# Casting transfers for the first quarter of w_in and for v of batches 3 to 7 in an attention-then-MLP kernel

## The chip, the cores and the metric

The kernel runs on one core of one Trainium2 chip. The metric is the device time of one execution in microseconds (us). Three executions of the kernel before took 284.15, 283.83 and 285.68 us, with a median of 284.15. Batches are counted from 0 here, as in the code: the "fourth to eighth batch" are b = 3 to 7.

The engines have short names in the profile: PE is the matrix engine (PEld its weight loads), DVE the vector engine, ACT the scalar engine, POOL the GpSimd engine, SP the engine that only issues transfers. A q behind a name (SPq, POOLq) is the sequencer of that engine.

## The reference

Eight batches of linear attention with cosine weights, and then an MLP on the result:

```python
def phi(x, c, s):
    r = np.maximum(x, 0.0)
    return np.concatenate([r * c, r * s], axis=-1)   # 64 -> 128 features
q_p, k_p = phi(q, cos_w, sin_w), phi(k, cos_w, sin_w)
kv  = np.einsum('bhsf,bhsd->bhfd', k_p, v)
z   = np.sum(k_p, axis=2)
num = np.einsum('bhsf,bhfd->bhsd', q_p, kv)
den = np.einsum('bhsf,bhf->bhs', q_p, z)[..., None] + 1e-06
x   = (num / den) as 4608 rows of 512
h   = x @ w_in                # 512 x 2048
g   = np.maximum(0.01 * h, h)
out = g @ w_out               # 2048 x 512
```

q, k and v are (8, 8, 576, 64) in f32, the weights and the output are f32 too.

## The kernel before

All matrix products are done in f16, so every input is cast on the way: q and k by the multiplication with cosine or sine that makes them qp and kp, v by a plain copy, the weights either by a copy or by the transfer itself. A transfer can cast only where it is issued from POOL here; those from SP bring f32 into a staging tile, and an engine casts from there.

The work is cut into nine groups of 512 rows: group g below 8 holds the first 512 positions of batch g, group 8 the last 64 positions of all batches. A group goes through these steps: its q becomes qp (`q_prep`, line 345), qp is transposed (`q_transpose_dma`, 362), the batch's k becomes kp (`k_cos`, `k_sin`, lines 282 and 285), v is copied into `vm`, PE sums kp times v (`kv_sum`, 316), PE multiplies with qp (`num`, 393), DVE divides, the rows are transposed (`x_transpose_dma`, 375), and then come the two layers of the MLP. From group 4 on (F7) the first layer, and from group 1 on (G7) the second, are done as seven products of quarter matrices in place of eight; the sums of quarters that this takes are `w1_sum` (569, of w_in), `x_sum` (585, of the rows), `weight_sum` and `g_sum`.

`vm` is one tile, `[128, 4, 9, 66]` in f16. It holds v of the current batch, 64 columns, beside two columns of ones. It may be written again only when `kv_sum` of the batch before has read it. Its casts are written by `v_pairs` (303), two of two head pairs each for a batch, on the engine that a letter in the schedule names.

Each engine takes its instructions in the order in which the program gives them, and waits at the head of its queue. That order is written out by hand up to group 1. After that a table, `TUNE`, gives every step a position in units of the stream of MLP products (16 a group); `weave` (897) puts the steps in at their positions. In this table, 'L' is for the loads of q, k and two halves of v, 'q' for `q_prep`, 'qT' for the transposes, 'kc' and 'ks' for `k_cos` and `k_sin`, 'v' for `v_pairs`, 'mm' for `kv_sum`, 'n' for `num`, 'x' for the transpose of the rows, and 'e' names the engines (A, D, P; S is POOL with a multiplication by one). 'W' and 'X' are for `w1_sum` and `x_sum`.

In the seven-product form the first layer of a group goes through PE in four units (`ffn1s`, 609), each as products 1, 5, 6, 2, 7, 3, 4. Product 5 needs the row sum X1, product 6 needs X2, product 4 needs X4. For group 4 the table puts X1 at 47.03 (DVE), X3 at 47.13 (DVE), X2 at 47.24 (POOL), the weight sum W3 of the second half at 48.2 (POOL) and X4 at 49.45 (POOL). `kv_sum` of batch 5 stands at 47.03.

Staging tiles for q, k and v come from a pool of four, in turn; k of batches 1 and 3 lies in `wext` and v of batch 1 in `ext`, which later hold sums of weights and of g. At the start SP issues q, k and v of batch 0 and then the first quarter of w_in (columns 0 to 511) into staging; POOL and DVE cast that quarter (`cast_w1`, 818). POOL issues the other three quarters of w_in, w_out, and q, k and v of batches 1 and 2. SP issues the loads of batches 3 to 7, the transposes and the stores.

Of the kernel before, what the change touches and what calls it, by code (L numbers as in the profile page):

```python
# [13 lines left out]
P = 128  # L14
J = 4

T = 9
# [3 lines left out]
def kernel(  # L21
# [14 lines left out]
    nc = tc.nc  # L36
    B, H, S, D = q.shape
# [10 lines left out]
    NKC = DM // P  # L48
# [33 lines left out]
    st = {}  # L82
# [6 lines left out]
    def need(*keys):  # L89
        for key in keys:  # L90
            assert key in done, key
# [7 lines left out]


    wext = const.tile([P, 3080], dt.float32, name="wext")
    in_wext = {("k", 1), ("k", 3)}

    def stage_tile(nm, i, a, b, d):
        if (nm, i) in in_wext:
            return wext[:, 0 : a * b * d].rearrange("p (a b d) -> p a b d", a=a, b=b)
        if (nm, i) in in_ext:
            lo = NS * in_ext[nm, i]
            return ext[:, lo : lo + a * b * d].rearrange(
                "p (a b d) -> p a b d", a=a, b=b  # L110
            )
        return stage.tile([P, a, b, d], dt.float32, name=f"{nm}st", tag="stage")
# [15 lines left out]
    def load_kv(nm, src, b, parts=(0, 1), eng=nc.sync):  # L128
# [9 lines left out]
            st[nm, b][:, sl].rearrange("p c j d -> p c (j d)"), rows[:, sl]  # L138
        )

    def load_qtail(i):
        t = stage.tile([P, H, D], dt.float32, name="qtl", tag="stage")
        for o in range(2):
            nc.sync.dma_start(
                t[o * TAIL : (o + 1) * TAIL],
                q[2 * i + o, :, MAIN:S, :].rearrange("h p d -> p h d"),
            )
        st["qt", i] = t
# [14 lines left out]

    def load_w1(i, c, n):

        sl = slice(c, c + n)
        if i > 0:
            t, lo = w1[i, c]
            POOL.dma_start(t[:, lo : lo + n], w1v[:, sl, 512 * i : 512 * (i + 1)])  # L169
            return  # L170
        if c == 0:
            st["w1", i] = stage_tile("w1", i, 1, NKC, 512)[:, 0]
        nc.sync.dma_start(st["w1", i][:, sl], w1v[:, sl, 512 * i : 512 * (i + 1)])

    def load_w2(i, lo=0, hi=4):
        POOL.dma_start(w2[:, 4 * i + lo : 4 * i + hi, :], w2v[i, :, lo:hi])
# [3 lines left out]
    for part in range(2):  # L180
        load_kv("k", k, 0, (part,))
        load_kv("v", v, 0, (part,))
    w1_parts = [(0, 0, 1), (0, 1, 1), (0, 2, 2)]
    for part in w1_parts:
        load_w1(*part)

# [72 lines left out]
    def copy(eng, o, i):  # L259
        if eng is ACT:  # L260
            nc.scalar.copy(o, i)
        else:
            eng.tensor_copy(o, i)
# [18 lines left out]
    def k_cos(b, j, eng, lo=0, hi=H // 2):  # L282
        k_token(b, j, eng, cos_t, 0, lo, hi)
# [283 lines left out]
        )  # L567

    def w1_sum(bp, n, eng):
        need(("kv", 3), *(("W", bp, i) for i in {1: (), 2: (1,), 4: (2,), 3: (1,)}[n]))  # L570
        if n == 3:
            need(("f1", F7 - 1))
        done.add(("W", bp, n))
        a11, a12, a21, a22 = (w1_quarter(bp, r, d) for r in range(2) for d in range(2))
        o1, o2, o4 = (SW[i][:, bp] for i in (1, 2, 4))
        if n == 1:
            tt_op(o1, a21, a22, ALU.add, eng)
        elif n == 2:
            tt_op(o2, o1, a11, ALU.subtract, eng)
        elif n == 3:  # L580
            tt_op(a21, a11, a21, ALU.subtract, eng)
        else:
            tt_op(o4, a12, o2, ALU.subtract, eng)
# [231 lines left out]
        else:  # L815
            nc.sync.dma_start(rows[:, tt, :], osb)

    def cast_w1(i, c, n, eng):
        t, lo = w1[i, c]
        copy(eng, t[:, lo : lo + n], st["w1", i][:, c : c + n])  # L820

# [12 lines left out]
    q_transpose(0, 1, ACT)  # L834
    idle(1)
    v_pairs(0, 0, 1, ACT)
    v_pairs(0, 1, 2, ACT)
    q_transpose(0, 2, ACT, "n")
    idle(1)
    q_transpose(0, 3, DVE)  # L840
    idle(6)
    kv_sum(0, 0, 2, "h")
    for j in range(7):
        k_cos(0, j, POOL if j < 1 else ACT, 2, 4)
    for c in range(0, NKC, 2):
        load_w1(1, c, 2)
    k_pair_half(0, 2, sin_t, D)
    k_pair_half(0, 3, sin_t, D)
    num_half(0, 0, 0, "h")
# [5 lines left out]
    idle(6)  # L855
    x_transpose_half(0, 0, 0)
    kv_sum(0, 2, 4, "h")
    cast_w1(*w1_parts[0], POOL)
    cast_w1(*w1_parts[1], POOL)
    cast_w1(*w1_parts[2], DVE)  # L860
    for i in range(2, NB):
        for c in range(0, NKC, 2):
            load_w1(i, c, 2)
# [61 lines left out]
    def at(pos, f, *args):  # L925
        steps.append((pos, lambda: f(*args)))
# [66 lines left out]
    for m in range(6, NFT):  # L993
# [157 lines left out]
    for b, t in TUNE["B"].items():  # L1151
        e = [engines[c] for c in t["e"]]
        if t["L"] is not None and b < B:
            at(t["L"][0], load_main, "q", q, b)
            at(t["L"][1], load_kv, "k", k, b)
            if t["L"][2] == t["L"][3]:
                at(t["L"][2], load_kv, "v", v, b)
            else:
                for i in range(2):
                    at(t["L"][2 + i], load_kv, "v", v, b, (i,))  # L1160
        elif t["L"] is not None:
            for j in range(J):
                at(t["L"][j], load_qtail, j)
        for j in range(J):
            at(t["q"][j], q_prep, b, j, 0, H, e[j])
            at(t["n"][j], num, b, j)
        for jp in range(2):
            at(t["qT"][jp], q_transpose_dma, b, jp)
        at(t["x"], x_transpose_dma, b)
        if b < B:  # L1170
            at(min(t["kc"] + t["ks"]) - 0.01, kp_tile, b)
            for j in range(T):
                at(t["kc"][j], k_cos, b, j, e[4 + j])
                at(t["ks"][j], k_sin, b, j, e[13 + j])
            for i in range(2):
                at(t["v"][i], v_pairs, b, 2 * i, 2 * i + 2, e[22 + i])
            at(t["mm"], kv_sum, b, 0, NC, "n")

# [31 lines left out]
```

## Time and profile before

The profiled execution took 284.36 us; its span from first to last instruction is 282.5 us, at a mean granted PE clock of 0.985 of full speed.

| engine | busy us | share of the span | instructions |
|---|---|---|---|
| PE (matmul) | 269.0 | 95% | 2813 |
| PEld (weight loads) | 213.3 | 75% | 2813 |
| DVE | 194.0 | 69% | 398 |
| ACT | 180.3 | 64% | 310 |
| POOL | 106.1 | 38% | 94 |

Where PE is not busy, by stretches of ten us, with the clock that it was granted and the transfer engines' share (the packets' time over that of 16 engines; over 1 where packets overlap):

| stretch | PE busy | DVE busy | POOL busy | PE clock | transfers |
|---|---|---|---|---|---|
| 0 to 10 | 7.68 | 5.29 | 3.75 | 1.00 | 0.79 |
| 10 to 20 | 8.34 | 8.83 | 8.37 | 1.00 | 1.08 |
| 60 to 70 | 6.28 | 9.33 | 9.64 | 0.78 | 0.93 |
| 70 to 80 | 9.15 | 7.50 | 5.28 | 0.88 | 0.73 |
| 140 to 150 | 10.00 | 8.73 | 9.26 | 1.00 | 0.75 |
| 270 to 280 | 8.30 | 4.66 | 0.00 | 1.00 | 0.35 |

In each of the other twenty-two stretches up to 270 PE is busy for 9.55 us or more. The loads that matter, with the median time from issue to landing: q of a batch from SP 7.8 us (1024 KB, five of them), v from SP 6.8 us (1152 KB, four), q from POOL 15.0 us (two), quarters of w_in from POOL in pairs of row blocks 7.1 us (six), eight parts of the tail of q (`qtl`, in pieces of 64 elements) 3.4 us.

A timeline row reads: start, duration, engine, line, operation, output<-inputs, shape, count, and in brackets how long the engine had been idle before and what ended that.

### The profile page before, as it was taken

To read this page: it belongs to the slowest core of one execution; us is meant where nothing else is said; L and a number is where in the kernel's file an instruction comes from. 1 tells how busy PE (TensorE), PEld (TensorE's weight loads), DVE (VectorE), ACT (ScalarE), POOL (GpSimd) and SP (SyncE) were. 2 spreads that over 40 slices of the span, in tenths; PEclk is the share of its full clock that TensorE was granted. 3 is DMA by queue.
4 is the path that set the end of the run, shared out by engine and by line. 5 is a ranking of instruction groups with operands and counts; after the bars stand their busy time and mean duration, and the time that the engine had idled before them with its cause. 6 is when DMAs were issued, how large, how long until landed. Compare 5 with 4: busy or idle time off the path is not lost.

```text
span 282.5 us, 6858 instructions
## 1 busy us (share of the span) xinstructions
PE 269.0 (95%) x2813; PEld 213.3 (75%) x2813; DVE 194.0 (69%) x398; ACT 180.3 (64%) x310; POOL 106.1 (38%) x94
## 2 busy tenths in 40 slices
PE   6889999976999999999999999999999999999993
PEld 2575455534586667667999999999998899999983
DVE  4860096588766459586987798987798758745752
ACT  7846456592654566796599679967676566676500
POOL 3593230899422930330799483342303003000000
PEclk9999999996899999999999999999999999999998
DMA  7999999959859977979969894865296051100124
GB/s 230 372 173 180 291 344 371 383 141 261 311 120 171 369 232 224 196 246 251 274 214 252 208 266 156 174 126 148 77 187 150 2 115 57 57 32 31 61 67 111
DMA packets 74559, 53.92 MB, mean 191 GB/s; under 512 B 49312, under 2 KB 65184, under 8 KB 74528
## 3 DMA queue, kind: packets, MB, share of 16 engines
q1 hardware_dynamic: 69904, 42.47, 58.2%
q0 software_dynamic: 4016, 10.49, 14.1%
q10 hardware_dynamic: 608, 0.52, 0.6%
q8 instruction: 22, 0.36, 0.5%
q14 instruction: 9, 0.07, 0.1%
HBM read 36.70 MB, written 9.44 MB: 163 GB/s over the span
## 4 chain that ended last, share of the span: by engine, by line
PE 69%; DMA 16%; DVE 7%; POOL 3%; issue 2%; ACT 1%; SPq 1%; POOLq 0%; DVEq 0%
PE ps L735 30%; PE ps_f L628 20%; PE ps_h L476 11%; DMA vst<-in_v_dram 6%; DMA w<-in_moe_w_out_dram 6%; DMA kst<-in_k_dram 3%; PE ps_kv L328 3%; PE ps_num L402 3%; POOL w L169 1%; PE ps_f L735 1%; DVE qp L255 1%; DVE ext L528 1%; DVE kp L255 1%; ACT g L654 1%; DVE xs L418 1%
## 5 line engine op out<-in xcount | busy, mean ns | idle before, releaser
L735 PEld LDWEIGHTS <-g 128*128 128x128 f16 x640 | 61.8, 98 | 8.2 <-ACT g L484 0.6
L735 PE MATMUL ps<-w,g 128*128 128x256 f16 x496 | 64.8, 273 | 0.4 <-ACT g L484 0.4
L476 PE MATMUL ps_h<-xT,w 128*128 128x512 f16 (+1 forms) x272 | 61.4, 375 | 0.1
L484 ACT ACTIVATE g<-ps_h 128x1024 f16<-128x1024 f32 x32 | 32.2, 1023 | 26.8 <-PE ps_h L476 26.8
L476 PEld LDWEIGHTS <-w 128*128 128x128 f16 x272 | 29.9, 115 | 21.9 <-issue 2.1
L654 ACT ACTIVATE g<-ps_f 128x512 f16<-128x512 f32 x60 | 34.7, 597 | 8.5 <-PE ps_f L628 6.1
L628 PEld LDWEIGHTS <-w 128*128 128x128 f16 x320 | 34.6, 114 | 0.8
L628 PE MATMUL ps_f<-xT,w 128*128 128x256 f16 x240 | 33.3, 273 | 0.0
L735 PE MATMUL ps<-T,ext 128*128 128x256 f16 x240 | 32.1, 272 | 0.0
L628 PEld LDWEIGHTS <-wext 128*128 128x128 f16 x240 | 26.4, 113 | 1.1 <-issue 0.5
L735 PEld LDWEIGHTS <-ext 128*128 128x128 f16 x256 | 24.8, 98 | 3.1 <-issue 0.2
L528 DVE TENSOR_TENSOR ext<-g 128x512 f16<-128x512 f16 (+1 forms) x23 | 15.0, 657 | 12.5 <-ACT g L484 10.5
L255 POOL TENSOR_SCALAR kp<-kst,cos_t 128x256 f16<-128x256 f32 (+1 forms) x13 | 16.5, 1274 | 18.9 <-PE ps_kv L328 15.9
L528 DVE TENSOR_TENSOR y<-ps_f,s 128x512 f32<-128x512 f32 x20 | 13.8, 688 | 11.1 <-PE ps_f L628 9.0
L255 DVE TENSOR_SCALAR qp<-qst,cos_t 128x512 f16<-128x512 f32 (+1 forms) x18 | 7.9, 441 | 18.4 <-DMA qst<-in_q_dram 18.4
L528 DVE TENSOR_TENSOR ext<-ps,ext 128x512 f32<-128x512 f32 x16 | 11.0, 689 | 13.1 <-PE ps L735 12.0
L418 DVE TENSOR_TENSOR xs<-ps_num,rden 128x512 f16<-128x512 f32 x28 | 19.4, 691 | 1.0
L628 PE MATMUL ps_f<-X,wext 128*128 128x256 f16 x128 | 19.2, 272 | 0.2 <-ACT ps_f L642 0.2
L654 ACT ACTIVATE g<-y 128x512 f16<-128x512 f32 x20 | 12.6, 632 | 9.9 <-DVE y L528 9.9
L528 DVE TENSOR_TENSOR osb<-ps,ext 128x512 f32<-128x512 f32 x23 | 15.7, 685 | 3.8 <-PE ps L735 3.7
L646 ACT COPY u<-ps_f 128x512 f32<-128x512 f32 x20 | 11.7, 587 | 10.1 <-PE ps_f L628 10.1
L528 POOL TENSOR_TENSOR X<-xT,X 128x512 f16<-128x512 f16 x7 | 9.0, 1283 | 21.6 <-PE ps_f L628 14.7
(120 smaller groups left out, 460.0 us busy)
## 6 DMA issues: line engine op xcount, KB each, us to landing
out_dram<-osb SPq DMA_DIRECT2D x32, 256.0 KB, 3.0
qst<-in_q_dram SPq DMA_DIRECT2D x5, 1024.0 KB, 7.8
vst<-in_v_dram SPq DMA_DIRECT2D x4, 1152.0 KB, 6.8
kst<-in_k_dram SPq DMA_DIRECT2D x4, 1152.0 KB, 8.1
vst<-in_v_dram SPq DMA_DIRECT2D x4, 576.0 KB, 6.8
qst<-in_q_dram POOLq DMA_DIRECT2D x2, 1024.0 KB, 15.0
w<-in_moe_w_in_dram POOLq DMA_DIRECT2D x6, 256.0 KB, 7.1
w<-in_moe_w_out_dram POOLq DMA_DIRECT2D x3, 512.0 KB, 13.3
```

What stands on the lines that cost most here:

```text
L169: POOL.dma_start(t[:, lo : lo + n], w1v[:, sl, 512 * i : 512 * (i + 1)])
L255: eng.tensor_scalar(out=o, in0=i, scalar1=0.0, scalar2=col, op0=ALU.max, op1=ALU.mult)
L328: nc.tensor.matmul(ps[:, o, (c - lo) * NE : (c - lo + 1) * NE], lhsT=st["kp", b][sl, c, j, :], rhs=vm[sl, c, j, :], start=(j == 0), stop=( ...
L402: nc.tensor.matmul(ps[lo:hi, h // 4, (h % 4) * NE : (h % 4 + 1) * NE], lhsT=qpT[:, h, lo:hi], rhs=kv[b][:, h, :],)
L418: nc.vector.tensor_tensor(out=xs, in0=ps[:, :, 0 : 4 * NE].rearrange("p a (b e) -> p a b e", e=NE)[:, :, :, 0:D], in1=rden.rearrange("p (a ...
L476: nc.tensor.matmul(ps[:, m % 2, lo:hi], lhsT=w1[m // 4, c][0][:, w1[m // 4, c][1], m % 4 : 512 : 4], rhs=xT[:, lo // P : hi // P, c, :], s ...
L484: nc.scalar.activation(st["g", g][:, m - 1 : m + 1, :], ps, AF.Lrelu)
L528: eng.tensor_tensor(out=o, in0=a, in1=b, op=op)
L628: nc.tensor.matmul(ps[:, mi * HT : (mi + 1) * HT], lhsT=a[:, c, 2 * r0 + mi : 512 : 4], rhs=b[:, c], start=(n in (1, 5) and mi == 0 and c ...
L646: nc.scalar.copy(u1, B_)
L654: nc.scalar.activation(st["g", g][:, m : m + 2, r * HT : (r + 1) * HT], {"a": A, "c": y22, "e": E, "d": B_}[e].rearrange("p (m t) -> p m t ...
L735: nc.tensor.matmul(ps[:, tt], lhsT=a[:, i, tt * P : (tt + 1) * P], rhs=b[:, i], start=(first and i == 0), stop=(i == NPR - 1 and (apart or ...
```

## The change

In words:

- **w_in, first quarter.** It is no longer staged and cast. POOL issues it in two casting transfers of 512 x 512 elements straight into its f16 tiles, the first after POOL's share of batch 0's qp, the second after a copy of v. The three SP transfers and the three casts (two on POOL, one on DVE) go. `load_w1(1, ...)` moves up behind it.
- **v of batches 3 to 7.** `load_v` (new) issues four transfers a batch from POOL, one for each pair of heads, that cast f32 to f16 and write `vm` in place, 64 elements (256 bytes read, 128 written) at a time: 1152 pieces a transfer, 4608 a batch. They stand behind `kv_sum` of the batch before, at 13.94/14.44, 26.46/26.96, 40.16/40.66, 47.33/47.83 and 62.18/62.68. The staged loads of v from SP and ten copies go (by the letters of 'e': one on ACT, two on DVE, seven on POOL).
- **q of batch 3** is issued from POOL rather than SP, at the same position (2.08).
- k of batch 3 uses the staging pool rather than `wext`, so that `w1_sum` may start once batch 1 is done; the pool's turns change with it.
- At the start one copy of v moves from ACT to POOL and one `k_cos` from POOL to ACT.

```diff
-    in_wext = {("k", 1), ("k", 3)}
+    in_wext = {("k", 1)}
...
+    def load_v(b, part):
+        need(("kv", b - 1))
+        cs = slice(2 * part, 2 * part + 2)
+        for c in range(cs.start, cs.stop):
+            rows = v[b, 2 * c : 2 * c + 2].rearrange("h s d -> (h s d)")
+            POOL.dma_start(vm[:, c, :, 0:D], rows.rearrange("(p j d) -> p j d", p=P, j=T))
+        done.update(("v", b, c) for c in range(cs.start, cs.stop))
...
     def load_w1(i, c, n):
-        sl = slice(c, c + n)
-        if i > 0:
-            t, lo = w1[i, c]
-            POOL.dma_start(t[:, lo : lo + n], w1v[:, sl, 512 * i : 512 * (i + 1)])
-            return
-        if c == 0:
-            st["w1", i] = stage_tile("w1", i, 1, NKC, 512)[:, 0]
-        nc.sync.dma_start(st["w1", i][:, sl], w1v[:, sl, 512 * i : 512 * (i + 1)])
+        t, lo = w1[i, c]
+        POOL.dma_start(t[:, lo : lo + n], w1v[:, c : c + n, 512 * i : 512 * (i + 1)])
...
-    w1_parts = [(0, 0, 1), (0, 1, 1), (0, 2, 2)]
-    for part in w1_parts:
-        load_w1(*part)
...
-        need(("kv", 3), *(("W", bp, i) for i in {1: (), 2: (1,), 4: (2,), 3: (1,)}[n]))
+        need(("kv", 1), *(("W", bp, i) for i in {1: (), 2: (1,), 4: (2,), 3: (1,)}[n]))
...
-    v_pairs(0, 1, 2, ACT)
+    load_w1(0, 0, 2)
+    v_pairs(0, 1, 2, POOL)
+    load_w1(0, 2, 2)
+    for c in range(0, NKC, 2):
+        load_w1(1, c, 2)
...
-        k_cos(0, j, POOL if j < 1 else ACT, 2, 4)
-    for c in range(0, NKC, 2):
-        load_w1(1, c, 2)
+        k_cos(0, j, ACT, 2, 4)
...
-    cast_w1(*w1_parts[0], POOL)
-    cast_w1(*w1_parts[1], POOL)
-    cast_w1(*w1_parts[2], DVE)
...
-           6: {'L': [42.28, 44.22, 45.5, 45.5],
-               'e': 'ADAAPPPPDPDPADPADPDPAPPP',
+           6: {'L': [42.28, 44.22, 47.33, 47.83],
+               'e': 'ADAAPPPPDPDPADPADPDPAP',
...
-               'v': [58.06, 56.62],
+               'v': [],
...
-            at(t["L"][0], load_main, "q", q, b)
+            at(t["L"][0], load_main, "q", q, b, (0, 1), POOL if b == 3 else nc.sync)
             at(t["L"][1], load_kv, "k", k, b)
-            if t["L"][2] == t["L"][3]:
+            if b > 2:
+                for i in range(2):
+                    at(t["L"][2 + i], load_v, b, i)
+            elif t["L"][2] == t["L"][3]:
...
-            for i in range(2):
+            for i in range(2 if b < 3 else 0):
                 at(t["v"][i], v_pairs, b, 2 * i, 2 * i + 2, e[22 + i])
```

On POOL, the changed program has around group 4's row sums this order: X2, the four transfers of v of batch 6, the weight sum W3, X4. Before, W3 and X4 followed X2 directly.

More of the change, by code (lines that the diff above doesn't have):

```diff
@@ L816, in ffn2_out @@
             nc.sync.dma_start(rows[:, tt, :], osb)
-    def cast_w1(i, c, n, eng):
-        t, lo = w1[i, c]
-        copy(eng, t[:, lo : lo + n], st["w1", i][:, c : c + n])
     for hg in range(2):
```

24 rows, old and new, of the table TUNE are left out of this document.

## The prediction

> **What bounds the kernel now.** I read the table of engines first, then busy time by ten-us stretches, then the chain of waits over 36 to 84 us, then timelines. PE is busy 95% of the span and from 80 us to 275 us it has hardly a gap, so nothing taken off another engine there can shorten the run. What is left to win lies in the start (0 to 20 us) and in one hole, shown here in stretches of 2 us (columns: stretch, sum, then busy us and instructions of PE, PEld, DVE, ACT, POOL; PE clock, transfer share, GB/s).
>
> ```profile
> 60.00:62.00 2.00, 2.00 (x10) 0.82 (x8) 2.00 (x4) 2.00 (x5) 2.00 (x2) 1.00 0.25 52
> 62.00:64.00 2.00, 0.09 (x5) 0.10 (x4) 2.00 (x4) 1.12 (x2) 2.00 (x2) 1.00 1.20 213
> 64.00:66.00 2.00, 0.50 (x14) 0.25 (x13) 2.00 (x5) 0.00 (x0) 1.64 (x2) 0.91 0.89 230
> 66.00:68.00 2.00, 1.70 (x58) 1.62 (x58) 2.00 (x4) 0.00 (x0) 2.00 (x2) 0.50 1.01 352
> 70.00:72.00 2.00, 2.00 (x12) 0.90 (x10) 1.55 (x4) 0.00 (x0) 1.48 (x2) 0.50 0.98 203
> 72.00:74.00 2.00, 2.00 (x17) 1.04 (x15) 1.11 (x4) 1.42 (x2) 0.00 (x0) 0.89 0.99 378
> ```
>
> PE idles 1.91 + 1.50 + 0.30 = 3.7 us; then its clock is halved from 65.64 to 72.44 (worked out from the 0.91 and the 0.89). The chain shows what that costs: four `ps_h` products take 1.83 us at 68.08 but 0.88 at 73.43, the eight at 70.35 take 2.83 where two fours are 1.76, so 0.95 + 1.07 = 2.0 us. After it come two PE gaps of 0.35 and 0.49 (75.41, 78.19). What ends the hole is a chain that starts with a late v of batch 2:
>
> ```profile
> 38.87 0.38 SPq L123 DMA_DIRECT2D qst<-in_q_dram  x1
> 39.53 0.75 POOL L137 DMA_DIRECT2D vst<-in_v_dram  x1 [0.50 <-issue]
> ...
> 57.87 1.06 DVE L263 CAST vm<-vst 128x1152 f16<-128x1152 f32 x1 [2.46 <-DMA vst<-in_v_dram]
> ...
> 65.55 0.69 DVE L255 TENSOR_SCALAR kp<-kst,sin_t 128x256 f16<-128x256 f32 x1
> 66.30 1.78 PE L328 MATMUL ps_kv<-vm,kp 64*128 64x66 f16 x58 [1.49 <-DVE kp L255]
> ```
>
> DVE waits 2.46 us for v, then works without a break to 66.24, and `kv_sum(2)` starts. The first row is q of batch 3: SP issues it just before v of batch 2, and both share engines that are full (share 1.03 to 1.06, 343 to 384 GB/s from 35 to 56 us).
>
> **The change, part by part.**
>
> *q of batch 3 on POOL.* It now stands behind v of batch 2. Its 1024 KB at 363 GB/s take 2.9 us from what is ahead of v. Behind it on SP stood the four stores of group 0 (issued from 47.98, 9.8 us to landing), which now run sooner: part of them came after v (58 to 60 us still move 71 GB/s) and will come before it; I allow 0.7 us. Net v lands 2.2 us sooner (0 if all four stores change sides; 2.46, DVE's whole wait, if none). DVE's row of work moves up with it. POOL's kp, the other releaser (its last before the sum ends at 64.43), follows q of batch 2, which also loses its rival. So `kv_sum(2)` ends its wait 2.2 us sooner: **-2.2**. q of batch 3 itself lands about 59; its first reader before started at 64.78. Its issue costs POOL 1.02 us (below) in a wait of 3.10 us before 50.53: nothing.
>
> *The half clock after it.* The hole shrinks from 3.7 to about 1.5 us. At the start PE has a gap of 1.0 us (the wait of `ps_qt` on qp) and stays at 1.00, so a hole of 1.5 is nearer to that than to 3.7: I take the clock as kept. That would give back 2.0, but DVE then is what PE meets: DVE had waited only 1.05 and 0.82 us for PE's `num` at 70.39 and 73.47. I take **-1.5** (0 to -2.8, with both small gaps).
>
> *w_in's first quarter.* The transfer before cost 1024 KB either way. POOL's rows of w_in run at about 150 GB/s written (149 and 154 in 16 to 25 us), 300 read, against 358 to 383 on SP at 10 to 14, so the quarter takes 3.5 us rather than 2.8; but POOL issues at 8.66, behind its qp, instead of 12.28, so the stream behind it ends where it did (+0.7 to -0.5). Three casts go: two on POOL (1.18 us at 14.58), one on DVE (0.68). DVE's two `k_cos` at 14.22 took 1.06 us beside them and 0.86 for four alone at 44.43. PE waits there for DVE kp (15.34): **-0.2** (+1.5, if the transfers from 8.66 hold back k and v of batch 0, to -0.6).
>
> *v of batches 3 to 7.* The ten copies removed (POOL 1.15 to 1.40, DVE 0.75, ACT 1.15 us) lie beside a full PE: nothing. Issues come in place. POOL's issues before, by number of runs: 128 runs 0.56 us, 256 runs 0.72, 1024 runs (q) 0.94 and 1.11. A transfer of 1152 pieces has no row; nearest is q's mean, 1.02, so 4.1 us a batch (2.3 by the cheapest row; 6.1 with the 0.50 that passed idle ahead of v at 39.53). Who stands behind them in POOL's queue? For batches 3, 4, 5 and 7: qp of batch 3 (`kv_sum(2)` ends at 65.9, plus 4.1 and two times 2.97 at most: 76; transposed at 82.90 before), w_in sums and qp of batch 4 (94.64 + 4.1 + 2.12 + 3.98 + 2.12 = 107; DVE wanted the sum at 110.44, SP the qp at 112.33), kp of batch 5 (wanted at 132.70), X4 of group 5 (159.1 + 4.1 + 1.6 = 164.8; product 4 at 168.32): slack covers 4.1. For batch 6 it does not:
>
> ```profile
> 135.71 1.39 POOL L528 TENSOR_TENSOR X<-xT,X 128x512 f16<-128x512 f16 x1 [9.71 <-PE ps_f L628]
> ...
> 137.06 2.58 POOL L528 TENSOR_TENSOR w<-w,w 128x1024 f16<-128x1024 f16 x1
> ...
> 139.60 1.60 POOL L528 TENSOR_TENSOR X<-xT,X 128x512 f16<-128x512 f16 x1
> ...
> 141.33 0.60 PE L628 MATMUL ps_f<-X,w 128*128 128x256 f16 x4
> ```
>
> These are X2, W3, X4 and product 4. X4 ends at 141.20, PE reads it at 141.33: slack 0.13. The four issues go between X2 and W3 (their own wait, `kv_sum(5)`, ended at 134.03), so PE, in order, idles 4.1 - 0.13 = **+4.0** (1.2, with the cheapest issue and W3 and X4 at their unhindered 2.12 and 1.15; 6.0).
>
> *The clock after that.* A hole of 4.0 us with nothing in it is nearest to the one of 3.7: half clock for 6.8 us. There 4.66 us of `ps_h` lost 2.0, that is 43%; 6.8 us of dense products lose **+3.0** (0 if it holds).
>
> *v's transfer.* `qtl` moves 4096 pieces of 256 bytes; in 193 to 199 us the share is 0.76, in 199 to 201 0.11, so 4.8 us of all engines, 5.4 for 4608 pieces against 3.2 for v at 363 GB/s. Least room has batch 5: POOL issues from 118.3 to 122.4, PE sums at 132.70, and 123 to 126 has share 0.46: nothing. The Trainium skill, "DMA: Bandwidth & Descriptors", Specifications, puts line rate at transfers of 512 bytes or more, with a read-modify-write below. The direction agrees with `qtl` (218 GB/s); 128-byte writes are in no row.
>
> *Staging.* SP loses five v and one q; k and q find their buffers no later than before. `w1_sum`'s looser need moves no position. Nothing.
>
> Sum on this execution: 284.36 - 2.2 - 1.5 - 0.2 + 4.0 + 3.0 = 287.5. The execution lies 0.21 over the median of three, so 287.3 there.
>
> **Rivals.**
>
> *A, the forecast*, 0.40.
>
> *B, the clock holds at 141.* For it: halving needed a hole inside which PE did 0.59 us of work out of 4.3, and when it falls may depend on where the hole lies. Against: 4.0 is longer than the idle 3.7 that did halve it. Then 287.3 - 3.0 = 284.3. Chance 0.20. The Trainium skill, "TensorE: Matmul & The Clock Gate", What's actually happening, gives this too: the clock falls after an idle window of about 3.4 us, in windows that run freely, and few holes of 4.0 contain a whole one. The hole at 62 contained none that was quite idle, and the clock fell: the trace speaks for the looser reading.
>
> *C, faster.* Place: the same X4, with issues that cost little. With 0.56 us each and W3 and X4 unhindered the stall is 1.2 and the clock holds; the first hole gives all: 284.15 - 2.2 - 2.8 - 0.3 + 1.2, so 280.1. It is over the bound of one per cent as long as that stall stays under 2.4 us. For: issue time grows less than runs do (eightfold, times two). Against: 1152 is past the dearest row. Chance 0.14.
>
> *D, v's pieces are slow.* At twice `qtl`'s time a batch takes 10.8 us; with 2.9 of q of batch 6 beside it, v of batch 5 ends at 134 rather than by 130, `kv_sum(5)` waits 1.5, the transposes before group 4 queue behind, 2 more: 290.8. For: half of qtl's size on the writing side. Chance 0.16.
>
> *E, q's move frees nothing*, as the stream of w_in ends later by what q gave back: without 2.2 and 1.5, 291.0. [...] Chance 0.10.
>
> DVE can lengthen the issues: X4 beside a busy DVE took 1.60 for 1.15, which on 4.1 would be 5.7, inside the bounds. The Trainium skill, "SBUF", Door 1's warning on "DVE blocks DMA", says POOL cannot write descriptors while DVE holds the shared port. q at 35.81, beside a busy DVE, took 1.11 for 0.94 at 19.64, with DVE idle: far milder.
>
> **How the numbers follow.** Time 287.3. Range 281.0 to 291.5: from the upper half of C to past E; below lie 0.07, above about 0.1. One per cent (2.8 us, about what can be told here) puts the bounds at 281.3 and 287.0. A lies within 286 to 289, 0.27 of its 0.40 above 287.0. Slower: 0.27 + 0.16 + 0.10 = 0.53; same: 0.13 + 0.20 = 0.33; faster 0.14.
>
> **What would show it.** Right: v of batch 2 cast by DVE near 55.7, `kv_sum(2)` started near 64; four POOL issues of about 1 us between X2 and W3; PE waiting for POOL X about 4 us at 138 (141 less what was won), then a clock of 0.50. Wrong: X4 done before PE wants it; a `kv_sum` waiting for a transfer (D); DVE's cast still at 57.9 (E); PE gaps elsewhere.

## The result and the profile after

| | runs | median us | range us |
|---|---|---|---|
| before | 4 | 284.5 | 283.83 to 285.68 |
| changed | 4 | 297.51 | 293.94 to 298.84 |

The ratio is 1.037, with a 95% interval of 1.027 to 1.046: the change makes the kernel slower. The medians lie 13 us apart, where 3 were forecast. A second measurement of the same two kernels, below, gave 1.045 (1.034 to 1.056). Ratios in this document leave out executions more than 1.5% above the fastest of their kernel, so where the waits of a kernel come and go the range of its times is given beside the ratio.

The profiled execution of the changed kernel took 293.94 us, 9.58 more than that of before; its span is 292.2 us, its mean granted clock 0.977 (0.985 before). Most lines have moved by one: the matmuls of `kv_sum` are L327, `phi_half` (qp and kp) is L254, `tt_op` (sums of two arrays) L527, `ffn2s` (the second layer) L734, and L146 is `load_v`.

The first hole, in the stretches of 2 us of the changed kernel (columns as in the prediction):

```profile
60.00:62.00 2.00, 1.81 (x12) 0.78 (x10) 2.00 (x5) 2.00 (x5) 2.00 (x2) 1.00 0.84 155
62.00:64.00 2.00, 0.00 (x0) 0.00 (x0) 2.00 (x5) 0.74 (x1) 2.00 (x2) 0.98 0.46 70
64.00:66.00 2.00, 1.23 (x46) 1.23 (x48) 2.00 (x3) 0.00 (x0) 1.07 (x2) 0.50 0.99 362
66.00:68.00 2.00, 2.00 (x33) 1.11 (x29) 0.07 (x1) 1.13 (x3) 2.00 (x3) 0.50 1.09 269
```

It is still there, and the clock still falls to a half behind it. But DVE, which ended it before, is now early: in 66 to 68 it is busy for 0.07 us. Who ends it is in the chain of waits over the same time (start, duration, what):

```profile
39.26 14.47 DMA vst<-in_v_dram
53.73 4.54 POOL qp L254 x2
58.26 6.47 POOL kp L254 x3
64.73 0.05 issue
64.78 2.05 PE ps_kv L327 x68
```

v of batch 2 landed earlier, as forecast (DVE casts it at 55.23, before at 57.87); POOL's kp took DVE's place. Then come holes that the kernel before does not have. What PE waited for between 55 and 270 us, as total, times and longest (the second row is the first hole again):

```profile
PE ps L734 <- DVE osb L527: 3.6, 1, 3.6
PE ps_kv L327 <- POOL kp L254: 3.0, 1, 3.0
PE ps_f L627 <- POOL X L527: 2.9, 1, 2.9
PE ps_f L627 <- DMA xT<-xs: 1.7, 1, 1.7
PE ps_num L401 <- DMA qpT<-qp: 0.6, 1, 0.6
```

Of these only the third is in the sum of the forecast. The timeline at that place answers to the prediction's X2, W3 and X4:

```profile
142.00 4.04 POOL L146 DMA_DIRECT2D vm<-in_v_dram  x4
...
143.55 2.10 DVE L527 TENSOR_TENSOR g<-g 128x1024 f16<-128x1024 f16 x1
...
146.06 2.13 POOL L527 TENSOR_TENSOR w<-w,w 128x1024 f16<-128x1024 f16 x1
...
148.15 1.15 POOL L527 TENSOR_TENSOR X<-xT,X 128x512 f16<-128x512 f16 x1
...
149.35 1.01 PE L627 MATMUL ps_f<-X,w 128*128 128x256 f16 x4 [2.91 <-POOL X L527]
```

Four issues of 1.01 us stand between X2 and W3, and PE waits for X4. (The DVE row comes up again at run 12.) The largest wait, near 104, is this one (timeline, rows of other lines left out):

```profile
98.19 2.00 POOL L254 TENSOR_SCALAR qp<-qst,cos_t 128x512 f16<-128x512 f32 x1
...
100.18 1.99 POOL L254 TENSOR_SCALAR qp<-qst,sin_t 128x512 f16<-128x512 f32 x1
...
100.88 5.73 DVE L527 TENSOR_TENSOR ext<-ext,g 128x512 f16<-128x512 f16 x1
...
102.14 2.11 POOL L527 TENSOR_TENSOR wext<-wext,w 128x1024 f16<-128x1024 f16 x1
...
104.22 2.11 POOL L527 TENSOR_TENSOR wext<-w,w 128x1024 f16<-128x1024 f16 x1
...
108.32 1.01 PE L734 MATMUL ps<-T,ext 128*128 128x256 f16 x4 [3.58 <-DVE osb L527]
```

In the kernel before, the same two instructions do not meet:

```profile
99.03 2.12 POOL L528 TENSOR_TENSOR wext<-w,w 128x1024 f16<-128x1024 f16 x1
...
102.93 0.41 DVE L528 TENSOR_TENSOR ext<-ext,g 128x512 f16<-128x512 f16 x1
```

A DVE sum that takes 0.41 us there takes 5.73 and ends at 106.61, just after POOL's last instruction of a row without a gap (106.33). Before, the same POOL row ran from 89.80 to 101.15; the four issues for v of batch 4 (92.03 to 96.06, behind a wait for `kv_sum(3)`) pushed it back by some 5 us, onto DVE's sums.

PE executes the same 2813 matmuls in the same order in both kernels, so the start of each can be compared. How far the changed kernel is behind the one before:

| place (us, changed) | what | step | behind, after it |
|---|---|---|---|
| 65 to 104 | start, first hole | -2.05 | -2.05 |
| 108.3 | DVE's sum, above | +3.57 | +1.52 |
| 108.3 to 111.5 | half clock | +1.52 | +3.04 |
| 140.2 | xT of group 4 late | +2.02 | +5.06 |
| 149.4 | X4 late | +2.96 | +8.02 |
| 149.4 to 152.5 | half clock | +1.50 | +9.52 |
| 181.3 | qpT late | +0.82 | +10.34 |
| to the end | | -0.33 | +10.01 |

### The profile page after: what moved, and what is told of

Same layout as the page of the kernel before. It is cut to its first block, busy times and chain, and to the rows that moved or that the text cites. A ratio compares the mean times of both kernels' runs of the same rounds, so it can differ in the third digit from the quotient of the medians.

```text
span 292.2 us, 6860 instructions
## 1 busy us (share of the span) xinstructions
PE 272.9 (93%) x2813; PEld 215.1 (74%) x2813; DVE 197.5 (68%) x395; ACT 179.4 (61%) x309; POOL 119.4 (41%) x108
## 4 chain that ended last, share of the span: by engine, by line
PE 59%; DMA 22%; DVE 8%; POOL 7%; issue 3%; ACT 1%; SPq 0%; POOLq 0%; DVEq 0%
PE ps L734 27%; PE ps_f L627 18%; PE ps_h L475 8%; DMA vst<-in_v_dram 7%; DMA qst<-in_q_dram 5%; DMA qpT<-qp 4%; DMA w<-in_moe_w_in_dram 3%; DVE ext L527 3%; PE ps_kv L327 2%; PE ps_num L401 2%; POOL kp L254 2%; DMA xT<-xs 2%; POOL qp L254 2%; PE ps_f L734 1%; POOL vm L146 1%
## 5 line engine op out<-in xcount | busy, mean ns | idle before, releaser
L734 PEld LDWEIGHTS <-g 128*128 128x128 f16 x640 | 61.8, 98 | 8.3 <-ACT g L483 0.6
L734 PE MATMUL ps<-w,g 128*128 128x256 f16 x496 | 64.8, 273 | 0.4 <-ACT g L483 0.4
L734 PE MATMUL ps<-T,ext 128*128 128x256 f16 x240 | 33.9, 283 | 3.6 <-DVE osb L527 3.6
L734 PEld LDWEIGHTS <-ext 128*128 128x128 f16 x256 | 25.7, 101 | 7.5 <-issue 3.8
L146 POOL DMA_DIRECT2D vm<-in_v_dram x20 | 20.5, 1026 | 21.6 <-PE ps_kv L327 21.6
L254 POOL TENSOR_SCALAR kp<-kst,cos_t 128x256 f16<-128x256 f32 x14 | 18.8, 1349 | 14.0 <-PE ps_kv L327 13.9
L527 DVE TENSOR_TENSOR y<-ps_f,s 128x512 f32<-128x512 f32 x20 | 13.8, 688 | 11.3 <-PE ps_f L627 9.1
L527 DVE TENSOR_TENSOR ext<-g 128x512 f16<-128x512 f16 (+1 forms) x23 | 13.9, 607 | 11.1 <-ACT g L483 9.1
L527 DVE TENSOR_TENSOR ext<-ps,ext 128x512 f32<-128x512 f32 x16 | 11.1, 691 | 15.2 <-PE ps L734 12.3
L254 DVE TENSOR_SCALAR qp<-qst,cos_t 128x512 f16<-128x512 f32 (+1 forms) x18 | 8.8, 488 | 18.5 <-DMA qst<-in_q_dram 18.5
L527 DVE TENSOR_TENSOR osb<-ps,ext 128x512 f32<-128x512 f32 x23 | 15.8, 685 | 5.1 <-PE ps L734 5.1
L527 DVE TENSOR_TENSOR ext<-ext,g 128x512 f16<-128x512 f16 (+1 forms) x23 | 18.2, 793 | 0.8
```

Of the source, the lines that this page charges most:

```text
L146: POOL.dma_start(vm[:, c, :, 0:D], rows.rearrange("(p j d) -> p j d", p=P, j=T))
L254: eng.tensor_scalar(out=o, in0=i, scalar1=0.0, scalar2=col, op0=ALU.max, op1=ALU.mult)
L527: eng.tensor_tensor(out=o, in0=a, in1=b, op=op)
L734: nc.tensor.matmul(ps[:, tt], lhsT=a[:, i, tt * P : (tt + 1) * P], rhs=b[:, i], start=(first and i == 0), stop=(i == NPR - 1 and (apart or ...
```

## The experiments

Theories at the start. *T*: the issues of v delay POOL's later work, and beside the X4 of the prediction the harm lies where that late work meets DVE (near 104) and where the pieces meet transposes. *Rivals*: the pieces or their descriptors hold DVE; the holes come and go by chance; the gain of q and w_in was never there.

**1. v of batch 4 staged.** `L` and `v` of batch 4 and the engines of its casts as before.

```diff
-            if b > 2:
+            if b > 2 and b not in {4}:
...
-           4: {'L': [16.71, 21.32, 26.46, 26.96], 'v': [],
+           4: {'L': [16.71, 21.32, 20.14, 20.14], 'v': [32.65, 35.2],
```

> v of batch 4 comes by SP into a staging buffer again and is cast by DVE and POOL, all else as changed. Theory (POOL's row of w_in sums and qp, pushed some 6 us back by the four issues, meets DVE's sums of g, and one DVE sum that reads two arrays is held until that row ends): the DVE sum that took 5.73 us takes 0.4 to 0.7, PE does not wait at 104, the 3.41 us of half clock there go; 5.1 us less than the changed kernel, so 288.8 beside its profiled 293.94, ratio to the kernel before about 1.015 where the changed one has 1.037. Rival 1 (chance: the DVE sum was held by something that comes and goes between executions): hole stays or the ratio stays at 1.037. Rival 2 (v4's transfers or descriptors held DVE, not POOL's row): the same as the theory here; the next run tells it apart.

Measured: ratio 1.034 (1.027 to 1.041), profiled 294.29. The sum took 0.41 us at 104.83 and the wait for `osb` is gone, as expected. The time did not follow, and the ratio stayed near the changed kernel's, which was a sign of rival 1: in this execution `kv_sum(2)` ended early, and PE then waited 5.16 us for qpT from 69 to 74.5, with 6.83 us of half clock. Neither theory had this cost; it is the subject of runs 5 and 11.

**2. The issues replaced by memsets.** As 1, with POOL clearing v's array (overwritten by the casts later) where the issues stood.

```diff
+    def hold(b):
+        need(("kv", b - 1))
+        for c in range(NC):
+            POOL.memset(vm[:, c, :, 0:D], 0.0)
...
+            if b == 4:
+                at(26.46, hold, b)
```

> As the run with v of batch 4 staged, but in the place of the four issues POOL clears v's array by four memsets after kv_sum(3), each about 1 us, so POOL's row comes late as in the changed kernel, with no transfer of small pieces in it. Theory (lateness of POOL's row): the hole at 104 is back, a DVE sum of g takes over 3 us and ends with POOL's row, PE waits 2 to 4 us; within 2 us of the changed kernel, ratio 1.030 to 1.037. Rival 2 (transfers or descriptors): no DVE sum over 1 us, no hole at 104, ratio about 1.015 as with v4 staged.

Measured: ratio 1.035 (1.027 to 1.042). The four memsets took 2.13 us in all, half of what the issues take. The wait for `osb` is back, with 2.14 us; DVE's sums took 1.47 and 2.34 us, a kp 1.23 instead of 0.35, and each ended within 0.3 us of the end of a POOL instruction. (This execution, of 297.57 us, was the longest of four.) So lateness of POOL's row does it without any transfer of pieces; "over 3 us" was too much for half the delay. The ratio cannot tell 1 from 2 here, as both had the wait for qpT.

**3. v of batch 6 behind X4.**

```diff
-           6: {'L': [42.28, 44.22, 47.33, 47.83],
+           6: {'L': [42.28, 44.22, 49.5, 49.51],
```

> The four issues of v of batch 6 stand behind X4 of group 4 in POOL's queue instead of ahead of W3 and X4, all else as changed. Theory (they alone delay X4): PE's wait of 2.91 us for X4 at 146 goes, and with it the 3.41 us of half clock behind it: 4.5 us less than the changed kernel, 289.4 beside 293.94, ratio 1.021 where that has 1.037. Rival (POOL is late at 146 from earlier, or the issues now hold up another POOL result): X4 still waited for, or a new wait for POOL after 150; under 2 us gained.

Measured: ratio 1.030 (1.023 to 1.037), profiled 291.98. PE no longer waits for X4 and there is no half clock near 150; nothing later waits for POOL. The other waits stayed: `osb` 3.6, xT 1.6, and 4.2 us in two waits for qpT. The mechanism is as the theory has it, but the gain in the ratio is less than half of what it said. In this profile the waits for qpT were longer (0.6 in the changed kernel's) and so was the half clock behind the hole for `osb` (6.83 us for 3.41).

**4. All of v staged**, with q of batch 3 and w_in as changed: `L`, `v` and casts of batches 3 to 7 as before, k of batch 3 in `wext` again.

> v of batches 3 to 7 staged and cast as before; what is left of the change is w_in's first quarter by POOL and q of batch 3 on that queue. Theory (these two are the gain, v's issues the whole loss): the changed kernel was 2.05 us ahead of the kernel before at 76 to 104 us, so 282.3 where that has 284.4, ratio 0.993. Rival (q's move frees nothing, the lead came from v of batch 3 going to POOL): ratio 0.998 to 1.002.

Measured: ratio 0.986 (0.982 to 0.990), 278.62 us (277.74 to 279.80): faster than both kernels, by more than expected. In the stretches of 2 us the first hole is hardly there, and the clock stays full:

```profile
60.00:62.00 2.00, 1.55 (x11) 0.61 (x9) 2.00 (x5) 2.00 (x4) 2.00 (x2) 1.00 0.94 160
62.00:64.00 2.00, 1.80 (x71) 1.51 (x72) 2.00 (x3) 0.99 (x3) 2.00 (x2) 1.00 1.02 373
```

So the two smaller parts gain some 4 us, and v's transfers cost some 5% against that.

**5. v of batch 3 alone** by POOL (batches 4 to 7 staged).

> Of v, only batch 3 comes in POOL's transfers, batches 4 to 7 staged and cast; w_in and q as changed. The kernel with all of v staged took 278.6 (ratio 0.986). Theory (v3's pieces, issued the moment kv_sum(2) ends, hold up the transposes of batch 2's qp issued just before; with v4 staged these were waited for 5.2 us at 69 and the clock halved for 6.8 us): PE waits 2 to 5 us for qpT near 69 and the clock falls, 5 to 8 us more than all staged, ratio 1.004 to 1.015. Rival (that wait was chance of one execution, or came from elsewhere in that kernel): within 1 us of all staged, ratio 0.986 to 0.990.

Measured: ratio 0.990 (0.985 to 0.995), 281.18 us (277.74 to 284.62). The profiled execution, one of the longer ones, shows it in the timeline:

```profile
61.20 5.10 SPq L364 DMA_TRANSPOSE qpT<-qp  x1
...
63.20 4.05 POOL L146 DMA_DIRECT2D vm<-in_v_dram  x4 [0.76 <-PE ps_kv L327]
...
73.61 0.62 PE L401 MATMUL ps_num<-kv,qpT 128*128 128x66 f16 x8 [4.36 <-DMA qpT<-qp]
```

The transposes are issued at 61.20 and v's pieces from 63.20; the transposes land 12.4 us after their issue, where the longest landing of them in this stretch is 7.5 us in the kernel before and 7.7 with all of v staged. Half clock of 6.83 us follows. On the ratio the expectation missed: the wait is not in every execution, as the range shows.

**6. v of batch 4 alone.**

> Of v, only batch 4 comes in POOL's transfers. Theory (POOL's row pushed back onto DVE's sums of g; stall 3.6 and half clock 1.5 in the changed kernel, 2.1 and 1.5 with memsets in the issues' place): PE waits 2 to 4 us for DVE's osb some 99 to 108 us in, 3.5 to 5 us more than all staged, ratio 0.998 to 1.004. Rival 1 (the collision needs the lateness that v3's issues add): no wait there, ratio 0.986 to 0.990.

Measured: ratio 1.002 (0.997 to 1.008): the theory. PE waits 3.1 us for `osb`. DVE and POOL in the timeline:

```profile
98.12 2.33 DVE L254 TENSOR_SCALAR kp<-kst,cos_t 128x256 f16<-128x256 f32 x1
...
98.18 2.11 POOL L527 TENSOR_TENSOR wext<-wext,w 128x1024 f16<-128x1024 f16 x1
...
100.25 2.17 POOL L527 TENSOR_TENSOR wext<-w,w 128x1024 f16<-128x1024 f16 x1
...
100.37 2.33 DVE L527 TENSOR_TENSOR ext<-g 128x512 f16<-128x512 f16 x1
```

Twice a DVE instruction of 0.35 to 0.43 us takes 2.33 and ends within 0.3 us of the end of a POOL instruction. The sum ahead of them, which took 5.73 us in the changed kernel, takes 1.31 here and ends with POOL's qp, at 98.2.

**7. v of batches 5 and 7 alone.**

> Of v, only batches 5 and 7 come in POOL's transfers. In the changed kernel PE waited 1.73 us for xT near 138 and 0.8 for qpT near 180; the first is there with all of v staged too (1.7 at 128). Theory (nothing behind these issues on POOL, only the transposes a little later): 0.8 to 1.5 us more than all staged, ratio 0.988 to 0.992. Rival (v5's pieces beside q of batch 6 delay the transposes as v3's do): PE waits over 3 us for xT, half clock behind it, ratio over 0.996.

Measured: ratio 0.997 (0.991 to 1.003), 278.66 to 286.83. PE waits 2.3 us for xT near 134, with 3.41 us of half clock behind it, and 0.6 for qpT near 173. This lies between the two: the wait is under the rival's 3 us, the half clock and the ratio are the rival's. The profiled execution, the longest of ten, also had 2.6 us of wait for POOL's kp at 62, which has nothing to do with these batches.

**8. v of batch 6 alone**, its issues ahead of W3 and X4.

> Of v, only batch 6 comes in POOL's transfers, ahead of W3 and X4 as in the changed kernel. Theory (stall 2.9 and half clock 1.5 as there): 4.5 us more than all staged, ratio 1.002, PE waiting for POOL X about 3 us. Rival (the stall of 2.9 came in part from POOL being late already): under 2 us, ratio under 0.993.

Measured: ratio 0.996 (0.992 to 1.000). PE waits 3.0 us for X4, with 3.41 us of half clock, so the stall does not come from earlier lateness; the ratio lies between the two.

**9. q of batch 3 alone**, on the kernel before.

```diff
-            at(t["L"][0], load_main, "q", q, b)
+            at(t["L"][0], load_main, "q", q, b, (0, 1), POOL if b == 3 else nc.sync)
```

> The kernel before with one thing changed: q of batch 3 on POOL's queue, behind v of batch 2. Both parts together (all of v staged) gave ratio 0.986, with no half clock and a first hole of 0.7 us. Theory (q's move is the gain, as the prediction has it: 2.2 for the earlier v and 1.5 for the clock): v of batch 2 cast at about 55, PE's hole near 62 under 1.5 us, ratio 0.986 to 0.990. Rival (w_in's quarter is the gain): v of batch 2 cast at about 57.9 and ratio over 0.996.

Measured: ratio 0.989 (0.984 to 0.994). v of batch 2 is cast at 55.48, DVE waits 0.85 us for it instead of 2.46. Near 62 PE still waits 2.0 us, over the 1.5 expected, for POOL's kp, with 3.41 us of half clock; the fastest execution (277.24) has a clock of 1.00. The gain is q's.

**10. w_in alone**: run 4 with q of batch 3 on SP.

> The kernel before with w_in's first quarter by POOL's casting transfers only (q of batch 3 on SP, v staged). Theory: the start gains 0 to 0.6 us, the hole near 62 stays as before (3.5 to 3.8 us, with half clock): ratio 0.996 to 1.000. Rival: ratio under 0.992.

Measured: ratio 0.998 (0.994 to 1.002): nothing that can be told. v of batch 2 is cast at 57.04 and DVE waits 2.42 us for it.

**11. v of batch 3 alone, issued later.**

```diff
-           3: {'L': [2.08, 11.11, 13.94, 14.44],
+           3: {'L': [2.08, 11.11, 20.0, 20.01],
```

> As the run with v of batch 3 alone by POOL, but its four issues stand behind POOL's qp and kp of batch 3, so that they start some 5 us later, when the transposes of batch 2 have landed. Theory (the pieces hold up the transposes that are under way when they come): the wait of 4.4 us for qpT near 69 goes and the clock holds, ratio 0.986 to 0.988, no issue on SP longer than before. Rival (any piece traffic between 60 and 76 delays these, or the wait moves to the next transposes at 75): a wait for qpT or xT over 2 us, ratio over 0.990.

Measured: ratio 0.986 (0.979 to 0.993), and no wait for qpT. The issues now come at 70.15. The transposes land sooner, which does not depend on when PE wants them (shortest, median and longest, in run 5 and here):

```profile
DMA to landing us min/median/max: 4.7/5.9/12.4
DMA to landing us min/median/max: 4.3/5.2/7.1
```

All profiles agree: the longest landing of these transposes is 10.8 to 13.2 us in the six where v of batch 3 is issued as `kv_sum(2)` ends, and 6.9 to 9.1 in the other thirteen. (This execution also had 2.7 us of wait for POOL's kp.)

**12. v of batch 4 alone, w_in's sums first.** The same issues and pieces, POOL's three sums ahead of them.

```diff
-     'W': [[31.24, 32.96, 34.8, 47.53], [37.35, 38.58, 38.89, 48.2]],
+     'W': [[26.3, 26.31, 34.8, 47.53], [26.32, 38.58, 38.89, 48.2]],
```

> As the run with v of batch 4 alone by POOL, but the three w_in sums on POOL stand ahead of the four issues instead of behind them. The same pieces and issues at the same time. Theory (DVE's sum of two arrays of g was held by POOL's late row of sums): no DVE sum over 1.7 us between 90 and 110, no wait for DVE's osb there, ratio 0.986 to 0.990 where v of batch 4 alone has 1.002. Rival (the issues or the pieces of v hold DVE): PE's wait for osb stays at 2 to 4 us, ratio 0.998 to 1.004.

Measured: ratio 0.990 (0.984 to 0.995), where the other order has 1.002; the wait for `osb` is gone. One part of the expectation missed, and in a telling way:

```profile
88.75 2.12 POOL L527 TENSOR_TENSOR wext<-w,w 128x1024 f16<-128x1024 f16 x1
...
89.14 2.28 DVE L527 TENSOR_TENSOR ext<-g 128x1024 f16<-128x1024 f16 x1 [5.37 <-ACT g L483]
```

The last of the sums now meets another DVE sum, of 0.69 us before, and holds it for 2.28. PE waits 1.35 us for DVE a little later, for the same reason as before at another place. At this place pieces and issues are not what holds DVE; POOL's sums are. Issues are not without effect everywhere. The sum that follows here took 1.06 us instead of 0.69 beside them. And beside the issues of v of batch 6, with nothing else on POOL, a DVE sum that takes 0.69 us alone took 1.77 to 2.12 in all five profiles that have it (143.55 in the changed kernel); PE did not wait for it.

**13. The changed kernel with three moves** in POOL's queue: `L` of batch 3 from 11, `W` from 12, `L` of batch 6 from 3. All of v still comes in pieces.

> The changed kernel with three moves in POOL's queue and nothing else: v3's issues behind POOL's qp and kp of batch 3, the three w_in sums ahead of v4's issues, v6's issues behind X4. Every transfer of v is still in 64-element pieces. Theory (the named causes are the whole loss): left are the wait for xT (1.6 to 2.5 us near 133, perhaps half clock behind it) and 0.8 us for qpT near 174, so 2 to 4 us over all staged (0.986): ratio 0.993 to 1.000. Rival (transfers in pieces cost more than these waits, everywhere): ratio over 1.010.

Measured: ratio 0.999 (0.995 to 1.004), as the theory said; the changed kernel has 1.037 and 1.045. But three of its 12 executions took 290.5 to 292.9, and by the medians of all executions the ratio is 1.002. What PE waited for:

```profile
PE ps_f L627 <- DMA xT<-xs: 2.7, 1, 2.7
PE ps L734 <- DVE ext L527: 1.6, 2, 1.2
PE ps_num L401 <- DMA qpT<-qp: 1.4, 2, 1.2
```

**14. The same, with q of batch 6 loaded behind the transposes of group 4** (`'L': [44.13, 44.22, 49.5, 49.51]`).

> As 'repaired', with q of batch 6 loaded by SP behind the transposes of group 4 instead of ahead of them. Theory (xT is late because q6's transfer and v5's pieces stand before it): xT waited for under 1 us, ratio 0.988 to 0.994. Rival (v5's pieces alone delay it): the wait stays at 1.6 to 2.5 us and the ratio is that of 'repaired'.

Measured: ratio 0.996 (0.992 to 1.001). There was no wait for xT, but 2.6 us for qpT in two waits, and 1.7 for DVE's xs. The wait named went, and others took some of its place; the intervals of 13 and 14 overlap.

**15. All of v staged, with q of batch 6 late.**

> All of v staged, with q of batch 6 behind the transposes of group 4. Theory: no wait for xT (all staged showed 1.7 us in its profile, other kernels with v5 staged none), 0 to 1.7 us gained: ratio 0.980 to 0.986. Rival (q6 now comes late for its qp, or k6 and the stores behind it do): ratio over 0.988.

Measured: ratio 0.988 (0.983 to 0.994), no wait for xT. That is no gain over run 4 and at the rival's bound, though the profile shows no wait for qpT; PE waited 3.0 us for POOL's kp near 62 here. Of the profiles with v of batch 5 staged only run 4's had the wait for xT.

**16. One kp of batch 2 from POOL to ACT**, on run 4.

```diff
-               'e': 'PDPDDDPPDADDDPPDAAAADADD',
+               'e': 'PDPDDDAPDADDDPPDAAAADADD',
```

> All of v staged (ratio 0.986), and the last of POOL's four kp of batch 2 moved to ACT. Theory (what is left of the hole near 62 is POOL's kp, lengthened by DVE's sums, 0.7 to 3.0 us): no wait for POOL's kp over 1.3 us, no half clock near 65, 0.5 to 2.5 us less than all staged, ratio 0.978 to 0.985. Rival (ACT, or DVE's kp, is next and as late): kv_sum(2) waits for ACT or DVE instead, ratio 0.985 to 0.990.

Measured: ratio 0.983 (0.979 to 0.988), 278.88 us: the fastest ratio, not to be told from run 4's. In the profiled execution v of batch 2 was late (DVE waited 2.39 us), PE waited 1.9 us for POOL's kp in two waits, and the clock halved for 3.41 us. What sets the last of this hole is not settled by it.

**17. The changed kernel again.**

> The changed kernel once more, unchanged. Theory: where POOL's kp of batch 2 end early (kp sin of 1.57 us instead of 3.13) kv_sum(2) ends near 63, v3's issues follow at once and PE waits 3 to 5 us for qpT near 69, with half clock after it; the holes for DVE's osb near 104, xT near 138 and X4 near 146 are there in any case. Profiled time then 296 to 300. Rival (these waits are as much a matter of chance as the first): one of the three later holes is missing.

Measured: 296.32 us (293.91 to 299.18), ratio 1.045. Here `kv_sum(2)` ended early (PE waited 1.0 us for POOL's kp; the kp sin took 3.13 us again, but began 2.1 us sooner), and PE waited 2.6 us for qpT instead, less than the 3 to 5 expected of that order. The three later holes are the same: `osb` 3.6 (DVE's sum took 5.75), xT 1.6, X4 3.0. The profiled time, 293.91, was not 296 to 300. What makes its other executions longer by 2 to 5 us was not seen in a profile.

## Why the prediction was wrong

The direction was right; the size was not, and the range ended 6 us under the median. Step by step:

- *q of batch 3, -2.2, and the half clock behind it, -1.5*: right in their sum. Alone, q's move gives 0.989, some 3.2 us of 283.4. That POOL's kp "follows" was not right: in the profile of the changed kernel POOL's row of qp and kp began 2.0 us sooner (48.52 for 50.53) but took 16.2 us for 13.9, with a kp sin of 3.13 us for 1.29 beside DVE's sums. So `kv_sum(2)` starts 1.5 us sooner, not 2.2, and the clock still falls, while with all of v staged it starts 4.1 us sooner. Of the 17 profiles with q on POOL nine have a kp sin of 3.13 us, and in six of them the clock fell at this hole; in the eight with 1.29 to 1.57 it never did. So "the clock as kept" holds in some executions only, and that the sum came out near is in part luck. Rival E, that the move frees nothing, is out.
- *w_in, -0.2*: not to be told from nothing (run 10).
- *The issues of v6, +4.0*: right in place and kind, mis-sized. The issues took 4.04 us as forecast (4.1), but W3 took 2.13 and X4 1.15 us, not the 2.58 and 1.60 of the row of before. 4.04 - 0.90 - 0.13 gives 3.0; measured 2.9 to 3.0 in the profiles of the changed kernel and runs 8 and 17.
- *The half clock behind it, +3.0*: mis-sized. It lasted 3.41 us, not 6.8, and cost 1.5. Rival B, that it holds, is out (runs 8 and 17, too).
- *"Slack covers 4.1" for batches 3, 4, 5 and 7, and v's transfer "nothing"*: this is the step that failed. For batch 4 its sum was right on its own terms: POOL's row did end at 106.33, before DVE and SP wanted its results. It asked who waits for POOL's results, and not what POOL's row runs beside; that DVE can lengthen POOL's work was in the prediction, the reverse was not. Moved by 5 us it ran beside DVE's sums of g and held one for 5.73 us: +3.6 and +1.5, the largest cost of all. Runs 2, 6 and 12 show that here it is POOL's own row, its sums above all, and neither issues nor pieces.
- For batch 3 the wait of the issues (for `kv_sum(2)`) sets their time, and that is just after the transposes of batch 2 were issued. Staged, v stands on SP's queue behind these transposes; on POOL's queue nothing holds it back. Their landing goes from 7.1 to 12.4 us (runs 11 and 5), which makes a wait of 2.6 us in the changed kernel itself (run 17) and up to 5.4 in kernels like it (run 2). For batches 5 and 7 transposes were late by 2.0 and 0.8 us; the wait for xT, of 1.6 to 2.7 us, is in every profile with v5 in pieces and q of batch 6 ahead of the transposes, and in one (run 4) with v5 staged. Rival D had v's pieces too slow and named the transposes, but for a `kv_sum` that waits for v; in no profile did a `kv_sum` wait for v in pieces.
- *Casts removed, nothing*: run 11, which drops two of them, has 0.986, as with all of v staged. The other eight have no run of their own, but no run shows a gain in v's part to set against its costs.

Taken alone the parts of v (batch 3, 4, 5 with 7, and 6) cost 0.4, 1.6, 1.1 and 1.0% over run 4, together 4.0 by the unrounded ratios; in the changed kernel it is 5.1 (1.037 against 0.986). With intervals of 0.4 to 0.9% on either side of each ratio the two sums can't be told apart. Three moves in a queue's order took back 3.8 of these by the ratio (run 13), with the spread noted there. What is left, about 1.3%, is with transposes that still land late, as far as the profiles of 13 and 14 show it; that was not taken apart further.

## What to carry to other kernels

When work is pushed later on a queue, slack against the readers of its results is half of the question: also list what it will now run beside, on an engine that it can hold up and on transfers under way. Look at the queue that a load leaves, too: moving a load to another queue takes away the order that the old queue gave it against everything else there. And where a part of a change removes only work that was hidden, any cost decides, so measure the parts apart; here the two small ones alone were 1.4% faster.

## What the hardware showed that was not expected

- *DVE and POOL hold each other up, by whole instructions.* A DVE sum of 0.41 us took 5.73 to 5.75 in three profiles (the changed kernel twice and run 3), over the rest of one POOL instruction and two whole ones behind it without a gap; in others sums took 2.28 to 2.34, to the end of one. It goes the other way, too: POOL's kp sin of batch 2 took 1.29 or 1.57 us in some profiles and 3.13 in others, beside DVE sums of 1.2 us. The Trainium skill, "SBUF — State Buffer", section "SBUF: two separate sides", has this as an exclusive lock that whichever starts first keeps for its whole instruction. The 2.28 to 2.34 agree; by that rule the 5.73 would have ended with POOL's qp at 102.17, and in the trace it did not get its turn between POOL's instructions. Nor does every such pair collide: the sum at 99.50 in the changed kernel took 0.43 beside POOL's qp (98.19 to 100.18).
- *Half clock comes in pieces of 3.41 or 6.83 us*, in all of the 25 times that the profiles have it between 50 and 265 us. The 19 PE holes of 2.75 us or more (from one matmul's start to the next, less its own time) all had it: the clock fell 1.9 to 4.5 us after the hole began. Of five lone ones from 2.17 to 2.71 three had it, of the lone ones up to 1.94 none. The Trainium skill, "TensorE: Matmul & The Clock Gate", section "What's actually happening", has free-running windows of about 3.4 us, which fits the lengths; that a whole window must be idle does not fit the 2.17 us in run 9.
- *A transfer of 1152 pieces of 128 bytes costs POOL 1.03 us to issue* (the mean of 20 in the changed kernel), no more than one of 1024 pieces of 1024 bytes (0.94 and 1.11 before), and lands 7.9 us later (the median).
